# Four late weight-gradient stores on the software DMA ring, cut into pieces of rows

## The chip, the cores and the metric

The kernel runs on one core of one Trainium2 chip. The metric is the time of one execution on the device in microseconds (us); lower is better. Three executions of the kernel before took 409.05, 408.28 and 407.12 us, a median of 408.28. One more execution was recorded by the hardware profiler and took 407.01 us.

A core has five engines with instruction streams of their own: PE (matrix products), DVE and ACT (elementwise work), POOL and SP (here almost only issuers of transfers). Transfers between the memory of the chip and the core's own memory (128 partitions, "rows" below) are carried by sixteen DMA engines, which all issuers share. A store that POOL issues goes through the software ring (q0 in the profile), one from SP through q1, one from ACT through q10.

## The reference, cut to what matters

The reference computes a gated mix of two branches for one token, and then all gradients of it:

```python
def _A_ref(x, k_cache, v_cache, wq, wo):          # H=32 heads, Sk=4096 keys, Dh=128, D=640
    q = (x @ wq).reshape(B, Sq, H, Dh).transpose(0, 2, 1, 3)
    scores = jnp.einsum("bhqd,bhkd->bhqk", q, k_cache) * (Dh ** -0.5)
    p = softmax(scores, axis=-1)
    o = jnp.einsum("bhqk,bhkd->bhqd", p, v_cache)
    return o.transpose(0, 2, 1, 3).reshape(B, Sq, H * Dh) @ wo

def _B_ref(x, w1, b1, w2):                         # F=1728
    h = x @ w1 + b1
    return (h * tanh(softplus(h))) @ w2

g = sigmoid((x * gate_w).sum(-1, keepdims=True))
out = g * _A_ref(...) + (1 - g) * _B_ref(...)
_out, _vjp = jax.vjp(_f, x, k_cache, v_cache, wq, wo, w1, b1, w2, gate_w)
return (out, *_vjp(grad_out))
```

All tensors are bf16. The caches K and V have 32 MB each, and their gradients dK and dV have as much: every byte of K and V is read once and every byte of dK and dV is written once. Beside them stand wq and its gradient dwq (640 x 4096), wo and its gradient dwo (4096 x 640), and the small second branch (w1, w2 and theirs). Each of dK, dV, dwq and dwo is an outer product of two vectors, so that the work is mostly moving bytes: 82.03 MB are read and 82.03 MB written.

## The kernel before, in words

The 32 heads are taken in 16 pairs (`NP`), and four pairs form a head group (`NG` = 4 groups of 8 heads). A pair's K is one tile of 128 partitions x 8192 elements (64 partitions for each head), and so is its V. There are seven such buffers (`bufs`, `kv0` to `kv6`). A V buffer is overwritten with dV in place, then stored, then free for the next load; a K buffer is treated in the same way. The list `loads` holds the loads in their order, and `pump` issues the next ones on SP's queue whenever a buffer is free. wq lies whole in one tile (`wqa`, 128 partitions x 5 x 4096: input row 5p + r lies in partition p), and dwq is written into it in place. wo is loaded one head group at a time into two buffers (`wob`, 128 x 8 x 640), and dwo is written over it.

The order of the work is written out by hand. The main loop runs over pairs i and, within a pair, over 16 slots s; `slot(i, s)` issues a fixed part of the attention work (transposes, products, softmax, the outer products `outer` on DVE and the stores `store_kv`), and then the functions that a table `side` holds for (i, s). `plan` and `at` fill that table. The store of dK goes out at slot 3 of the next pair and that of dV at slot 13: on POOL's queue as long as there are loads left, on SP's queue after that. The last pair (i = 15) is written out behind the loop: its dV and dK go out in halves on SP (`last_dv`, `last_dk`), dwo of the last head group in two halves on ACT.

What the change touches:

- `st_dwo(g, eng, ...)` stores dwo of a head group. For group 2 (the third), it is planned at pair 13, slot 0, on POOL (line 689): one store of 128 partitions, 10,240 bytes in each.
- `st_dwq(c0, c1, eng)` stores a range of columns of dwq. The columns of group 2 (1024 of them) go out at pair 14, slot 6, on POOL (line 702): 128 partitions with five runs of 2048 bytes each. The first 512 columns of group 3 go out at pair 15, slot 3, on POOL (line 709), and its last 512 columns behind the loop on POOL (line 902), between `last_dk(1)` and `last_dk(2)`: 128 partitions with five runs of 1024 bytes each.
- The three short outputs (`frow`, line 934) are issued last, on POOL too.

Four more things bear on the order in which POOL issues: its stream is served in order; every store waits for the engine that made its data; the ring's stores use eight completion semaphores in turn, so that a store also waits until the one eight places before it has landed; and loads on SP wait for the store that empties their buffer.

Of the kernel before, what the change touches and what calls it, by code (L numbers as in the profile page):

```python
# [17 lines left out]
def kernel(  # L18
# [33 lines left out]
    nc = tc.nc  # L52
    P = 128
# [8 lines left out]
    GC = 8 * Dh  # L62
# [10 lines left out]
    HC = 2 * GC  # L73
# [7 lines left out]
    dwq_v = out_4.rearrange("(p r) c -> p r c", r=RC)  # L81
    wo_v = A_wo.rearrange("(g p k) n -> g p k n", p=P, k=8)
    dwo_v = out_5.rearrange("(g p k) n -> g p k n", p=P, k=8)
# [24 lines left out]
    wqa = big.tile([P, RC, H * Dh], BF16, name="wq", tag="wq")  # L108
    wob = [big.tile([P, 8, D], BF16, name=f"wo{i}", tag=f"wo{i}") for i in range(2)]
# [242 lines left out]
    def dwo_row(g, k, eng=nc.scalar):  # L352
        scaled(eng, wob[g % 2][:, k, :], da_bc[:], o8f[:, k:k + 1])

    def st_dwo(g, eng, k0=0, k1=8):
        eng.dma_start(dwo_v[g][:, k0:k1], wob[g % 2][:, k0:k1])


    def kview(b):
# [127 lines left out]
    def dwq_row(g, c0, c1, rc, eng=nc.scalar):  # L487
        scaled(eng, wqa[:, rc, g * GC + c0:g * GC + c1], dqrow[g % 2][:, c0:c1], xf[:, rc:rc + 1])

    def st_dwq(c0, c1, eng):  # L490
        eng.dma_start(dwq_v[:, :, c0:c1], wqa[:, :, c0:c1])


    hT = C([P, FN], F32, "hT")
# [123 lines left out]
    def at(i, s, f, *a):  # L618
        side.setdefault((i, s), []).append(lambda: f(*a))

    def plan(i, table):
        for s, tasks in table.items():
            for t in tasks:
                at(i, s, *t)

    def dx(g, part, c0, c1, *rcs):
        return [(dx_sum, g, part, c0, c1, rc) for rc in rcs]
# [42 lines left out]
    for k in range(8):  # L670
        at(4, (6, 7, 9, 10, 11, 11, 13, 14)[k], dwo_row, 0, k, nc.vector if k in (4, 5, 6, 7) else nc.scalar)
    plan(4, {5: rows(mlp_dxb, 0), 7: rows(mlp_dxb, 1), 14: rows(mlp_dxb, 2)})
    plan(5, {0: [(st_dwo, 0, nc.gpsimd)], 1: [(ld_wo, 2)], 5: rows(mlp_dxb, 3), 7: rows(mlp_dxb, 4), 14: dx(0, 0, 0, GC, 0)})
    plan(4, {10: [(ld_wq, HC, 2 * HC, nc.scalar)]})
    plan(6, {0: [(st_dw1,)]})

    for g in range(NG - 1):
        i = 4 * g + 4
        if g:
            plan(i - 1, {14: [(o_dup, g)]})  # L680
            plan(i, {0: [(o_rows, g)], 2: [(a_cols, g, 0, 2)], 3: [(a_cols, g, 2, 4)], 4: [(a_cols, g, 4, 5)]})
            if g + 2 < NG:
                for k in range(8):
                    at(i, 5 + k // 4, dwo_row, g, k, nc.vector)
                plan(i, {7: [(st_dwo, g, nc.gpsimd)], 15: [(ld_wo, g + 2)]})
            else:
                for k in range(8):
                    at(i, (5, 6, 7, 9, 10, 12, 13, 14)[k], dwo_row, g, k)
                plan(i + 1, {0: [(st_dwo, g, nc.gpsimd)]})
        for k, (j, s) in enumerate((((1, 14), (2, 5), (2, 6), (2, 7), (2, 14)), ((1, 5), (1, 7), (2, 5), (2, 7), (2, 14)),  # L690
                                    ((0, 14), (1, 5), (1, 6), (1, 7), (1, 14)))[g]):
            if (g, k) != (0, 0):
                plan(i + j, {s: dx(g, g, 0, GC, k)})
            at(i + j, s + 1 if s < 15 else s, dwq_row, g, 0, GC, k)
    for g in (2, 3):
        i = 4 * g
        q_prep(i - 1, 2, g)
        plan(i - 2, {15: sums(g, 0)})
        plan(i - 1, {4: sums(g, 1), 5: sums(g, 2, 3), 6: sums(g, 4, 5), 7: sums(g, 6, 7)})
        do_prep(i - 1, 8, g)  # L700
    plan(12, {8: [(st_dwq, 0, HC, nc.scalar)]})
    plan(14, {6: [(st_dwq, HC, HC + GC, nc.gpsimd)]})

    CA, CB = GC // 2, 3 * GC // 4
    g, i = NG - 1, NP - 2
    for k, s in enumerate((5, 6, 7, 14, 15)):
        plan(i, {s: dx(g, g, 0, CA, k)})
        at(i, s + 1 if s < 15 else s, dwq_row, g, 0, CA, k)
    at(i + 1, 3, st_dwq, g * GC, g * GC + CA, nc.gpsimd)
    plan(i + 1, {4: dx(g, NG, CA, CB, 0, 1, 2), 5: dx(g, NG, CA, CB, 3, 4)})  # L710


# [144 lines left out]
    i, g = NP - 1, NG - 1  # L857
# [9 lines left out]
    def last_dk(t):  # L867
        outer(fb, st[i]["ds"], Qr[g % 2][:, q, :], t)
        if t % 2:
            h = slice((t - 1) * KVW // 4, (t + 1) * KVW // 4)  # L870
            nc.sync.dma_start(dKv[i][:, h], bufs[fb][:, h])
# [27 lines left out]
    for rc in range(RC):  # L899
        dx_sum(g, NG + g, CB, GC, rc)  # L900
        dwq_row(g, CB, GC, rc)
    st_dwq(g * GC + CA, (g + 1) * GC, nc.gpsimd)
    last_dk(2)
    last_dk(3)

# [58 lines left out]
```

## Time and profile before

| What | Value |
|---|---|
| Median of three runs | 408.28 us (407.12 to 409.05) |
| The profiled execution | 407.01 us, of which its instructions span 405.2 us |
| PE, DVE, ACT, POOL busy | 74%, 70%, 61%, 6% of the span |
| Bytes moved | 164.88 MB, 407 GB/s on average |
| Queue q1 (SP), share of the sixteen DMA engines' time | 55.7% |
| Queue q0 (POOL, software ring) | 37.4% |
| Queue q10 (ACT) | 4.0% |
| Third group's dwo (1280 KB), issued on POOL | 322.98 us |
| Third group's dwq (1280 KB), issued on POOL | 341.59 us |
| Fourth group's first half of dwq (640 KB), issued on POOL | 363.98 us |
| Fourth group's second half of dwq (640 KB), issued on POOL | 388.43 us |
| The short outputs (1.2 KB each), issued on POOL | 393.78 to 395.3 us |

The span runs from the first instruction to the last; around it lie 1.8 us of the execution's own time. The slices of the profile cut the span in 40 parts of 10.1 us and show each engine's busy share in tenths; its line "DMA" is the mean over the sixteen DMA engines, so that one engine busy alone shows as 0.06. A table by stretches has, behind the engines, the clock of PE, that mean share, and the GB/s moved. A line with "<-" names who ended a wait. "us to landing" is the time from the issue of a transfer until the last byte is reported. L and a number is a line of the kernel before.

### The profile page before, as it was taken

The page shows a single profiled execution, that of the slowest core. Times are in us where ns is not written, and L with a number is a line of the kernel's source. Part 1 is how long each engine was busy: PE and PEld are TensorE (multiplying, and loading weights), DVE is VectorE, ACT ScalarE, POOL GpSimd, SP SyncE. Part 2 cuts the span into 40 slices and gives each one's busy share as a digit, 9 for nine tenths or more (in the row PEclk, how much of TensorE's full clock was granted, in tenths as well). Part 3 has the DMA queues.
Part 4 walks back from the last instruction along what each step waited for, and adds up shares of the span by engine and source line. Part 5 has one row for each costly group of instructions (what it writes and reads, how often), then busy time and mean ns, then how long its engine had stood idle before and what let it go on. Part 6 is the DMA issues. An engine that isn't in the chain of part 4 may idle for free.

```text
span 405.2 us, 13019 instructions
## 1 busy us (share of the span) xinstructions
PE 301.1 (74%) x5643; PEld 278.8 (69%) x5646; DVE 285.5 (70%) x618; ACT 247.0 (61%) x507; POOL 25.1 (6%) x50
## 2 busy tenths in 40 slices
PE   3769898898886788792989879652989976787310
PEld 3548897877876778692789869652789776786200
DVE  2744969599984987864697949462695979497760
ACT  3444545477657778862667677651568996767520
POOL 3000000002000101000001000000000100000020
PEclk9886999899899889975999999895899999899555
DMA  8999999999999999999999999999999999999991
GB/s 263 429 401 429 422 421 420 429 413 362 389 427 427 415 415 426 424 432 424 432 432 420 430 425 426 429 422 437 428 425 407 424 426 421 415 432 416 387 412 61
DMA packets 15963, 164.88 MB, mean 407 GB/s; under 512 B 1713, under 2 KB 1905, under 8 KB 6178
## 3 DMA queue, kind: packets, MB, share of 16 engines
q1 hardware_dynamic: 8832, 94.08, 55.7%
q0 software_dynamic: 5472, 63.42, 37.4%
q10 hardware_dynamic: 1602, 6.56, 4.0%
q8 instruction: 44, 0.72, 0.7%
q14 instruction: 13, 0.11, 0.1%
HBM read 82.03 MB, written 82.03 MB: 405 GB/s over the span
## 4 chain that ended last, share of the span: by engine, by line
PE 29%; issue 24%; DMA 21%; DVE 15%; ACT 6%; POOL 2%; POOLq 0%; SPq 0%; ACTq 0%; DVEq 0%
PE tr L372 11%; DVE kv L463 7%; DMA out_dram<-kv 7%; DMA kv<-in_A_k_cache_dram 6%; DMA wo<-in_A_wo_dram 6%; PE dP L382 3%; PE dq L431 2%; PE S L382 2%; DMA wq<-in_A_wq_dram 2%; ACT tch L375 2%; PE o L431 2%; PE q_ps L275 2%; DVE junk L288 1%; PE a_ps L338 1%; PE h_ps L527 1%
## 5 line engine op out<-in xcount | busy, mean ns | idle before, releaser
L372 PE MATMUL tr<-idf,kv 128*128 128x128 f32 x1024 | 176.4, 300 | 33.9 <-DMA kv<-in_A_k_cache_dram 16.9
L375 ACT COPY tch<-tr 128x512 f32<-128x512 f32 x256 | 144.5, 587 | 82.9 <-PE tr L372 78.4
L372 PEld LDWEIGHTS tr<-idf,kv 128*128 128x128 f32 x1024 | 121.6, 153 | 40.7 <-issue 37.7
L382 PEld LDWEIGHTS <-tch 128*128 128x128 bf16 x2048 | 91.8, 100 | 24.8 <-ACT tch L375 19.8
L463 DVE TENSOR_TENSOR kv<-p_dup,Dr 128x2048 bf16<-128x2048 bf16 x64 | 76.6, 1219 | 4.6 <-ACT p_dup L422 4.2
L463 DVE TENSOR_TENSOR kv<-ds_dup,Qr 128x2048 bf16<-128x2048 bf16 x64 | 76.8, 1220 | 0.4
L431 PEld LDWEIGHTS <-kv 128*128 128x128 bf16 x2048 | 59.9, 98 | 6.0 <-issue 5.0
L382 PE MATMUL dP<-dR,tch 128*128 128x48 bf16 x1024 | 48.9, 187 | 8.8 <-ACT tch L375 8.4
L382 PE MATMUL S<-qR,tch 128*128 128x48 bf16 x1024 | 48.1, 187 | 6.1 <-ACT tch L375 5.3
L431 PE MATMUL dq<-ds_m,kv 128*128 128x48 bf16 x1024 | 31.2, 183 | 5.4 <-issue 2.9
L288 DVE SCALAR_TENSOR_TENSOR junk<-wo,da_bc 128x640 bf16<-128x640 bf16 x32 | 26.3, 822 | 11.3 <-DMA wo<-in_A_wo_dram 10.6
L431 PE MATMUL o<-e_m,kv 128*128 128x48 bf16 x1024 | 32.6, 187 | 0.0
L734 POOL DMA_DIRECT2D out_dram<-kv x25 | 13.4, 535 | 296.4 <-DVE kv L463 236.5
L350 ACT ACTIVATE wq<-dqrow,xf 128x1024 bf16<-128x1024 bf16 (+2 forms) x30 | 25.1, 860 | 1.2 <-DVE wq L484 0.8
L484 DVE SCALAR_TENSOR_TENSOR wq<-wq,dqrow 128x1024 bf16<-128x1024 bf16 (+2 forms) x30 | 25.1, 863 | 0.2
L437 DVE TENSOR_TENSOR o<-o,rz 128x2 f32<-128x2 f32 x16 | 2.5, 158 | 31.1 <-PE o L431 31.1
L422 ACT ACTIVATE p_dup<-e_m,rz 64x128 bf16<-64x128 bf16 x32 | 12.7, 397 | 7.8 <-DVE rz L416 7.4
L350 ACT ACTIVATE wo<-da_bc,o8f 128x640 bf16<-128x640 bf16 x20 | 15.9, 825 | 1.5 <-PE a_ps L338 1.0
L404 DVE TENSOR_REDUCE negM<-mt 64x1 f32<-64x64 f32 x32 | 7.1, 222 | 12.2 <-PE mt L401 11.6
L396 DVE TENSOR_REDUCE m<-S 64x1 f32<-64x64 f32 x32 | 7.0, 219 | 12.0 <-PE S L382 11.7
L478 PE MATMUL dqr_ps<-idb,dqb 128*128 128x128 bf16 x32 | 4.9, 240 | 13.1 <-DVE dqb L475 13.1
L457 ACT COPY ds_dup<-ds_m 64x128 bf16<-64x128 bf16 x32 | 9.5, 296 | 8.2 <-DVE ds_m L453 7.6
(161 smaller groups left out, 251.1 us busy)
## 6 DMA issues: line engine op xcount, KB each, us to landing
out_dram<-kv POOLq DMA_DIRECT2D x25, 2048.0 KB, 19.4
kv<-in_A_v_cache_dram SPq DMA_DIRECT2D x16, 2048.0 KB, 19.7
kv<-in_A_k_cache_dram SPq DMA_DIRECT2D x15, 2048.0 KB, 20.2
out_dram<-kv SPq DMA_DIRECT2D x5, 2048.0 KB, 26.2
wo<-in_A_wo_dram SPq DMA_DIRECT2D x4, 1280.0 KB, 21.1
out_dram<-kv SPq DMA_DIRECT2D x4, 1024.0 KB, 16.5
out_dram<-wo POOLq DMA_DIRECT2D x3, 1280.0 KB, 27.0
wq<-in_A_wq_dram SPq DMA_DIRECT2D x2, 1280.0 KB, 9.5
```

The lines of the kernel that those rows point to most:

```text
L275: nc.tensor.matmul(ps[:].rearrange("p a h d -> p (a h d)"), lhsT=xc[:, rc:rc + 1].to_broadcast([P, P]), rhs=wqa[:, rc, g * GC + a * 512:g ...
L288: nc.vector.scalar_tensor_tensor(junk[:], in0=wob[g % 2][:, k, :], scalar=1.0, in1=da_bc[:], op0=ALU.mult, op1=ALU.mult, accum_out=do8[g % ...
L350: nc.scalar.mul(dst, src, col)
L372: nc.tensor.transpose(tp[:, t, :], src[:, 4 * c + t, :], idf[:])
L375: nc.scalar.copy(dst[:].rearrange("p a b e -> p (a b e)").bitcast(F32), tp[:].rearrange("p a b -> p (a b)"))
L382: nc.tensor.matmul(ps[:, 4 * B:4 * B + W].rearrange("p (a b) -> p a b", b=4), lhsT=src[:, t, :, e], rhs=col[:, e, :, :].rearrange("p a b - ...
L422: nc.scalar.activation(p[HS[hh]], e_m[i % 2][HS[hh], :, hh].unsqueeze(2).to_broadcast([64, J, 2]), ACT.Copy, scale=st[i]["rz"][HS[hh], hh: ...
L431: nc.tensor.matmul(st[i][key][:].rearrange("p (a b) -> p a b", b=2), lhsT=src[:, j, :], rhs=rhs[:, j, :].unsqueeze(1).to_broadcast([P, W / ...
L457: nc.scalar.copy(ds[HS[hh]], ds_m[i % 2][HS[hh], :, hh].unsqueeze(2).to_broadcast([64, J, 2]))
L463: nc.vector.tensor_tensor(kview(b)[:, j0:j0 + n, :].rearrange("p j (a b) -> p j a b", b=2), col[:, j0:j0 + n, :].unsqueeze(2).to_broadcast ...
L484: nc.vector.scalar_tensor_tensor(w, in0=w, scalar=1.0, in1=dqrow[g % 2][:, c0:c1], op0=ALU.mult, op1=ALU.mult, accum_out=dq_acc[:, rc, par ...
L734: eng.dma_start(dst, bufs[b][:, 0:J * Dh])
```

## The change

`st_dwo` and `st_dwq` get an argument `rows`, a list of counts of partitions that add up to 128. They issue one store for each count, on the same queue, one after the other; together the pieces write the bytes that the one store wrote. Without the argument they do what they did. Four calls use it:

- dwo of the third group: 5, 120 and 3 rows
- dwq of the third group: 14, 105 and 9 rows
- the first half of dwq of the fourth group: 8 and 120 rows
- the second half: 9, 8, 105 and 6 rows

POOL thus issues twelve stores in place of four. Every other instruction is the same, and stands in the same order.

```diff
-    def st_dwo(g, eng, k0=0, k1=8):
-        eng.dma_start(dwo_v[g][:, k0:k1], wob[g % 2][:, k0:k1])
+    def st_dwo(g, eng, k0=0, k1=8, rows=(P,)):
+        p0 = 0
+        for n in rows:
+            eng.dma_start(dwo_v[g][p0:p0 + n, k0:k1], wob[g % 2][p0:p0 + n, k0:k1])
+            p0 += n
...
-    def st_dwq(c0, c1, eng):
-        eng.dma_start(dwq_v[:, :, c0:c1], wqa[:, :, c0:c1])
+    def st_dwq(c0, c1, eng, rows=(P,)):
+        p0 = 0
+        for n in rows:
+            eng.dma_start(dwq_v[p0:p0 + n, :, c0:c1], wqa[p0:p0 + n, :, c0:c1])
+            p0 += n
...
-                plan(i + 1, {0: [(st_dwo, g, nc.gpsimd)]})
+                plan(i + 1, {0: [(st_dwo, g, nc.gpsimd, 0, 8, (5, 120, 3))]})
...
-    plan(14, {6: [(st_dwq, HC, HC + GC, nc.gpsimd)]})
+    plan(14, {6: [(st_dwq, HC, HC + GC, nc.gpsimd, (14, 105, 9))]})
...
-    at(i + 1, 3, st_dwq, g * GC, g * GC + CA, nc.gpsimd)
+    at(i + 1, 3, st_dwq, g * GC, g * GC + CA, nc.gpsimd, (8, 120))
...
-    st_dwq(g * GC + CA, (g + 1) * GC, nc.gpsimd)
+    st_dwq(g * GC + CA, (g + 1) * GC, nc.gpsimd, (9, 8, 105, 6))
```

## The prediction, made before the changed kernel was run

> **What bounds the kernel now.** I read the span and the slices first, then the queues, then the issues of the four stores, then the last ten microseconds in steps of one, then what the ending waits for.
>
> ```profile
> span 405.2 us, 13019 instructions
> DMA  8999999999999999999999999999999999999991
> GB/s 263 429 401 429 422 421 420 429 413 362 389 427 427 415 415 426 424 432 424 432 432 420 430 425 426 429 422 437 428 425 407 424 426 421 415 432 416 387 412 61
> q1 hardware_dynamic: 8832, 94.08, 55.7%
> q0 software_dynamic: 5472, 63.42, 37.4%
> ```
>
> From the second slice to the last but one the sixteen DMA engines are over 90% busy and move some 420 GB/s, while PE, DVE and ACT are at 61 to 74% of the span: transfers set the pace. Only the last slice (395.1 to 405.2) is empty. By microsecond, with DMA share and GB/s as the last two columns:
>
> ```profile
> 394.00:395.00 1.00, 0.00 (x0) 0.00 (x0) 0.00 (x0) 0.00 (x0) 1.00 (x3) 0.50 1.03 395
> 395.00:396.00 1.00, 0.00 (x0) 0.00 (x0) 0.00 (x0) 0.00 (x0) 0.31 (x1) 0.50 0.78 298
> 396.00:397.00 1.00, 0.00 (x0) 0.00 (x0) 0.00 (x0) 0.00 (x0) 0.00 (x0) 0.50 0.37 149
> 397.00:398.00 1.00, 0.00 (x0) 0.00 (x0) 0.00 (x0) 0.00 (x0) 0.00 (x0) 0.50 0.21 83
> 398.00:399.00 1.00, 0.00 (x0) 0.00 (x0) 0.00 (x0) 0.00 (x0) 0.00 (x0) 0.50 0.07 25
> 402.00:403.00 1.00, 0.00 (x0) 0.00 (x0) 0.00 (x0) 0.00 (x0) 0.00 (x0) 0.50 0.06 25
> ```
>
> A share of 0.06 is one engine of sixteen, at 25 GB/s, and it is alone for over 5 us. SP's ending waits for it: first for the last dwq store, then 5.2 us more for a store of dK.
>
> ```profile
> SPq L959 <- DMA out_dram<-wq: 10.1, 1, 10.1
> SPq L959 <- DMA out_dram<-kv: 5.2, 1, 5.2
> ```
>
> The packet records of the trace name no engine, but a packet begins where the one before it on its engine ends, so that they can be laid into sixteen unbroken sequences. In these one engine is late: its last packet ends at 403.46, the next at 398.20, 397.83, 397.37 and 397.26, the other eleven by 396.5. At 391.3 it has 25 packets of 8 KB (205 KB) more to do on SP's queue than the engines that lead. It is slow all along: from 130 us its 16 KB packets take 654 ns on the software ring and 634 on SP's queue, against 613 to 622 and 611 to 620 on the others. The last landings, 0.4 us behind the packets, are 403.89 for it and 399.2 for the next. Its row sums agree: 25 stores of 128 rows left 3200 packets of 16 KB, thus 8 rows an engine, equal for all.
>
> The four stores, on POOL:
>
> ```profile
> 322.98 0.53 POOL L356 DMA_DIRECT2D out_dram<-wo  x1 [1.98 <-ACT wo L350]
> 341.59 0.85 POOL L491 DMA_DIRECT2D out_dram<-wq  x1 [18.08 <-ACT wq L350]
> 363.98 0.84 POOL L491 DMA_DIRECT2D out_dram<-wq  x1 [21.55 <-ACT wq L350]
> 388.43 0.82 POOL L491 DMA_DIRECT2D out_dram<-wq  x1 [23.61 <-ACT wq L350]
> 393.78 1.53 POOL L934 DMA_DIRECT2D out_dram<-frow  x3 [4.52 <-DVE frow L931]
> ```
>
> All lie in the last 83 us, and POOL waits in front of each.
>
> **The change, part by part.** No compute moves and no byte is added. Four issues become twelve, in POOL's order, at the same places.
>
> *Issues.* Two more at 323 (0.53 us each), two at 341.6, one at 364 and three at 388.4 (0.85 each at most): 5.3 us of POOL, which is 6% busy. The first three lie in POOL's own waits of 18.1, 21.6 and 23.6 us. The last group ends at 388.43 + 4 x 0.85 = 391.8, and frow is ready at 393.5: 1.7 us of cover. Without it each further issue would put out_0, out_1 and out_9 back by 0.85; they land at 400.3 by the records, 3.6 us ahead of the end. Each ring store also waits that the one eight before it has landed. The pieces bring that forward: the fourth piece at 388.4 waits for the first at 341.6, which in the kernel before landed as a whole by 367; frow's three wait for pieces issued by 364, landed by 378. Nothing. Nor does SP pass or meet a new wait: it loads and stores in the old order. **Sum: 0**, at most 1.
>
> *Who carries the rows.* The trace shows equal shares of 128 rows only; no store of 5, 105 or 120 rows is in it. Bounds: spread evenly (no effect); on few engines (a loss, below); or equal shares with a whole engine left out. Between them I take the row that is nearest, the 128 rows as 8 on each. 120 is 15 x 8 and 105 is 15 x 7: in equal whole shares each leaves one engine of sixteen out. If shares are dealt in turn, one engine after the other, the pieces ahead of the large ones (5; then 5+15+3+14 = 37; 37+15+9+8 = 69; 69+15+9+8 = 101) begin each large piece at the sixth engine from the start (5, 37, 69 and 101 are all 5 more than a multiple of 16). So all four large pieces leave out the same engine, the fifth. It gets 2, 2, 1 and 3 rows in place of 8. A row is 10.24 KB (dwo; dwq of 1024 columns) or 5.12 KB (512 columns): 6 x 10.24 + 6 x 10.24 + 7 x 5.12 + 5 x 5.12 = 184 KB less on it, and on average 184/15 = 12.3 KB more on each of the others, never above one row in a store (30.7 KB in all).
>
> *If the fifth is the late engine.* Relief: 184 KB at 25.1 GB/s (16 KB in 654 ns) = 7.3 us, so that it would land at 396.6. Then others are last: 399.2 plus 12.3 KB at 26.7 GB/s (16 KB in 614 ns) = 0.46, thus 399.7. The ending moves by 403.9 - 399.7 = **-4.2 us**. On the way the loads, which wait for stores to land in SP's queue (26 waits, 287.6 us in total), come up to 2.4 us earlier after the first store, but the other engines have no free time to use it in, save in the stretch from 380 to 384 (share 0.93 and 0.84, 0.46 us idle). The floor is perfect balance: the shares after 395 add up to 1.7 us of all engines, an end at 396.7 in place of 403.46, -6.7 us.
>
> *Sum.* The profiled execution took 407.01 (its span of 405.23 and 1.8 around it): 407.0 - 4.2 = 402.8. It lies 1.3 under the median of the three runs, 408.28; from the median 404.1, and with a little of the stretch at 380 **404.0 us**.
>
> [...]
>
> **The rivals.**
>
> *1. The engine left out is not the late one.* No view numbers the engines, so nothing excludes it. The late engine then keeps its 8 rows or gets one more in some stores: 0 to 30.7 KB, 0 to 1.2 us, on average 0.5. Time 408.3 to 409.5, likeliest 408.8: no change that can be measured (within 0.5%, 2.0 us, is about what a measurement of this kernel can't tell from none). For it: fifteen places out of sixteen are wrong ones, and the engine left out could differ from one execution to the next if the dealing goes on where the last one stopped (the pieces add up to 122, which is 10 over a multiple of 16). Against it: the amount left out, 184 KB, is near the 205 KB that the late engine is behind, sizes that agree only if the two have to do with one another.
>
> *2. Slower: the large pieces go on few engines.* That shape decides is shown: dwo in 128 rows went out 8 rows an engine, but the one-row store at L602 left a single packet of 3456 bytes. With 120 rows on eight engines and 105 on seven, each of these has 15 rows for 8: 7 x 10.24 x 2 + 7 x 5.12 x 2 = 215 KB more, 8.1 us. On engines that are not late: 399.2 + 8.1 = 407.3, +3.4, thus 411.7; with the late one among them +8.1, thus 416. It decides as soon as an engine has over 4.7 us (125 KB) too much. Against it: the 64-row store of dW2 went over all sixteen.
>
> *3. The tail moves, but less.* The late engine's relief at 323 and 341.6 is eaten by 388, since it gets new loads as soon as old ones land; only the last two stores' 61 KB (2.4 us) stay. Time 405.9. Against it: its backlog grows from stage to stage, which means that it keeps what it owes.
>
> **How the numbers follow.** The forecast 0.54, with its own range 402.0 to 405.5 (-6.3 to -2.8); rival 3 0.07; rival 1 0.26; rival 2 0.09; 0.04 for loss by pieces that I don't see, such as three more issues that put frow behind the end. The first is a judgement on one open question, which engine is left out; size speaks for it, numbering is silent. Faster by over 0.5% (under 406.2): 0.54 and most of rival 3, 0.60. Slower (over 410.3): rival 2, the rest and the top of rival 1, 0.14. Same: 0.26. The range goes from 401.8, under which I leave 0.03, to 410.0, over which I leave 0.15.
>
> **What would show it.** Right: in the last slices the DMA share falls from 1.0 to nothing within 3 us, no stretch of 0.06 over 2 us; SP's last wait for a dK store shrinks from 5.2 to about 1; landings of SP's loads after 345 come nearer to those of the other fifteen engines; POOL has twelve issues, all done by 392. Wrong: a tail of 0.06 as long as before (rival 1), or several engines busy after 400 (a share of 0.4, rival 2). The forecast fails if the dealing starts elsewhere or a piece is not dealt in whole equal shares.

## The result, and the profile after

The changed kernel takes 409.59 us (median of 20 runs, 407.01 to 412.43) against 407.88 for the kernel before (20 runs, 406.01 to 410.43): ratio 1.0053, 95% interval 1.0035 to 1.0071, thus some 2.2 us slower. The forecast was 404.0 us and faster. The range (401.8 to 410.0) holds the time; the direction is wrong. The first rival (408.3 to 409.5, the engine left out is not the late one) came nearest.

The page after, its slices and the two large queues:

```profile
span 406.2 us, 13027 instructions
DMA  8999999999999999999999999999999999999992
GB/s 281 422 410 429 429 414 426 426 428 423 424 426 409 392 423 427 424 431 431 431 423 428 426 429 422 429 423 433 427 393 387 423 422 412 424 393 382 384 386 85
q1 hardware_dynamic: 8832, 94.08, 55.9%
q0 software_dynamic: 5808, 63.42, 37.6%
```

The engines are as busy as before, but in the four slices ahead of the last they move 393, 382, 384 and 386 GB/s, where the kernel before had 432, 416, 387 and 412. All queues together were busy for 97.9% of 405.2 us, 396.7 us of each engine; now (55.9 + 37.6 + 4.1 + 0.7 + 0.1 = 98.4% of 406.2) for 399.7. The same 164.9 MB cost 3.0 us more.

The last microseconds after, DMA share and GB/s in the last two columns:

```profile
394.00:395.00 1.00, 0.00 (x0) 0.00 (x0) 0.00 (x0) 0.00 (x0) 0.93 (x2) 0.50 1.00 316
395.00:396.00 1.00, 0.00 (x0) 0.00 (x0) 0.00 (x0) 0.00 (x0) 0.00 (x0) 0.50 0.96 302
396.00:397.00 1.00, 0.00 (x0) 0.00 (x0) 0.00 (x0) 0.00 (x0) 0.00 (x0) 0.50 1.02 297
397.00:398.00 1.00, 0.00 (x0) 0.00 (x0) 0.00 (x0) 0.00 (x0) 0.00 (x0) 0.50 0.70 233
...
402.00:403.00 1.00, 0.00 (x0) 0.00 (x0) 0.00 (x0) 0.00 (x0) 0.00 (x0) 0.50 0.06 25
403.00:404.00 1.00, 0.00 (x0) 0.00 (x0) 0.00 (x0) 0.00 (x0) 0.00 (x0) 0.50 0.06 25
```

Two things stand here. The lone engine at 0.06 and 25 GB/s is still last. And from 394 to 397 all engines are busy at some 300 GB/s; before, a share of 1.03 at 394 moved 395. SP's ending waits for the same two stores as before, 13.1 and then 3.6 us (before 10.1 and 5.2): the others are later, the late one not earlier.

```profile
SPq L965 <- DMA out_dram<-wq: 13.1, 1, 13.1
SPq L965 <- DMA out_dram<-kv: 3.6, 1, 3.6
```

POOL's issues came as forecast, twelve stores in four groups, the last done 2.9 us ahead of the short outputs and with no wait between its pieces:

```profile
322.79 1.58 POOL L358 DMA_DIRECT2D out_dram<-wo  x3 [1.63 <-ACT wo L350]
341.48 2.10 POOL L496 DMA_DIRECT2D out_dram<-wq  x3 [17.11 <-ACT wq L350]
365.29 1.48 POOL L496 DMA_DIRECT2D out_dram<-wq  x2 [21.71 <-ACT wq L350]
387.95 2.56 POOL L496 DMA_DIRECT2D out_dram<-wq  x4 [21.19 <-ACT wq L350]
393.40 1.52 POOL L940 DMA_DIRECT2D out_dram<-frow  x3 [2.89 <-DVE frow L937]
```

**Who carried the rows.** The packet records bear out the shares: 31 packets of 1024 bytes, which is 8 + 9 + 8 + 6 (the small pieces of the fourth group's two dwq stores, one engine for each row), 38 of 2048 (14 + 15 + 9) and 15 of 3072 (the last store's piece of 105 rows, on fifteen engines). (A share of dwq went in packets of 4096 bytes, 602 of them on the ring, before 640, and a last one for the rest; these are the last ones.) An engine without rows in a piece was not passed over: for each packet that an engine with rows moved it ran a small one, of 4 to 16 bytes; besides 4 bytes for each engine and each of the eight more stores, the trace after has 75 more packets of 4 bytes than the one before, 35 more of 8, one of 12 and 51 of 16, in all 162, as many as that makes over the twelve pieces. But the engine that was left out was not the late one. The sixteen landings of dwo's 120 rows (us from the start of the span, as all times here):

```
339.56 342.34 342.61 342.76 343.21 343.34 343.35 343.87 344.00 344.09 344.32 344.81 344.89 345.19 346.23 351.74
```

339.56 is the engine without rows; 351.74 is the late engine, which had its eight. It is last in the stores of dK, dV and dwq from there on, and ends at 404.88 (before 403.89). In its sequence of packets at the end it has a row of the piece of 9, none of the 8, seven of the 105 and none of the 6. Followed back to 318 us, that is one of the places 10 to 12 of the dealing (counted from 0), not place 4 (the fifth). At these it carries one row of 10.24 KB more in all: 0.4 us.

**What the packets cost.** From the packet records, the time of the larger packets (1 KB and more), per KB, in the stretches of the late dwq stores, and the mean busy time of the sixteen engines over the whole execution:

```
                        356 to 380        392 to 404
kernel                  ring    SP queue  ring    SP queue   busy, us
before                  40.7    38.4      43.1    38.8       396.4
after                   53.3    41.3      55.3    44.2       399.5
after, once more        51.3    42.3      56.1    43.9       400.2
even pieces             55.1    39.7      59.1    45.3       399.9
halves of 64            56.1    41.3      66.0    42.2       401.0
halves of 64, again     55.2    41.8      67.4    41.8       402.6
every other row         40.3    38.5      45.0    39.0       395.8
halves by columns       40.6    38.5      44.9    39.5       396.7
                        (ns a KB)
```

The rows below "after" are experiments, told next. In the changed kernel, the even pieces and the halves of 64, the stores' own packets take 26 to 56% longer than before, and SP's packets beside them 3 to 17% longer.

### The profile page after: what moved, and what is told of

Same layout as the page of the kernel before. It is cut to its first block, busy times and chain, and to the rows that moved or that the text cites. A ratio compares the mean times of both kernels' runs of the same rounds, so it can differ in the third digit from the quotient of the medians.

```text
span 406.2 us, 13027 instructions
## 1 busy us (share of the span) xinstructions
PE 298.7 (74%) x5643; PEld 277.4 (68%) x5646; DVE 285.7 (70%) x618; ACT 247.2 (61%) x507; POOL 29.7 (7%) x58
## 3 DMA queue, kind: packets, MB, share of 16 engines
q1 hardware_dynamic: 8832, 94.08, 55.9%
q0 software_dynamic: 5808, 63.42, 37.6%
## 4 chain that ended last, share of the span: by engine, by line
issue 43%; DMA 18%; PE 17%; DVE 13%; ACT 4%; POOL 2%; POOLq 0%; SPq 0%; DVEq 0%; ACTq 0%
DMA kv<-in_A_k_cache_dram 11%; DVE kv L466 7%; PE tr L375 6%; DMA out_dram<-kv 5%; DMA wq<-in_A_wq_dram 2%; PE o L434 2%; POOL out_dram L740 2%; PE dP L385 1%; PE S L385 1%; ACT tch L378 1%; PE q_ps L275 1%; PE dq L434 1%; PE h_ps L533 1%; PE a_ps L338 1%; DVE wq L487 1%
## 5 line engine op out<-in xcount | busy, mean ns | idle before, releaser
L487 DVE SCALAR_TENSOR_TENSOR wq<-wq,dqrow 128x1024 bf16<-128x1024 bf16 (+2 forms) x30 | 25.1, 862 | 0.2
L412 ACT ACTIVATE e_m<-S,negM 64x64 bf16<-64x64 f32 x32 | 10.6, 330 | 6.8 <-DVE negM L407 6.1
```

The lines of the kernel that those rows point to most:

```text
L412: nc.scalar.activation(e_m[i % 2][HS[hh], :, hh], sview(S_ps[i], hh), ACT.Exp, bias=st[i]["negM"][HS[hh]], scale=1.0, accum_out=rs[i % 2][ ...
L487: nc.vector.scalar_tensor_tensor(w, in0=w, scalar=1.0, in1=dqrow[g % 2][:, c0:c1], op0=ALU.mult, op1=ALU.mult, accum_out=dq_acc[:, rc, par ...
```

## The experiments

Theory A: the late engine wasn't the one left out, and rows on the wrong engines are all that happened. Theory B: cutting a store by rows makes its packets slow by itself, whoever carries them. A third question is whether the relief would have worked, had it met the late engine.

**1. The changed kernel once more.**

> The changed kernel once more, for one more trace. In the first trace of it the packet records show the engine left out as the fifth from the start of the dealing, and the late engine as the eleventh, twelfth or thirteenth. If every execution begins the dealing at the same engine, the late engine is found in the same places again, and the tail of one engine at 0.06 is there again (about 4 to 6 us). If the dealing goes on from the execution before, the late engine is found elsewhere, the tail may be gone, and the time lies anywhere from 404 to 410 us.

One run: 407.57 us, span 405.7. The late engine is again not the one left out (of the 120 rows' landings the first is 339.76, the fifteenth 347.76 and the late one 350.65), and the last landing is 404.27. Its packets, followed back to 318 us, again fit the places 10 to 12 alone. So the miss is no single event.

**2. A probe of the dealing.** The last dwq store alone is cut:

```diff
-    st_dwq(..., nc.gpsimd, (9, 8, 105, 6))
+    st_dwq(..., nc.gpsimd, (2, 2, 2, 2, 2, 2, 2, 2, 3, 2, 2, 2, 2, 2, 99))
```

> A probe: the three earlier stores whole as before; the last dwq store alone is cut into 2 rows eight times, then 3, then 2 five times, then 99. Dealt in turn, the eight pairs go once round the sixteen engines, so that the trace shows in which pair the late engine stands: from the first trace of the change the sixth or seventh pair (places 11 to 13 of 16). If the dealing does not restart, any pair. Its time says little: fifteen issues at 0.85 us would put frow back to about 401, and 99 rows on eleven engines cost those up to 0.3 us: 407 to 412 us.

410.45 us (one run). The late engine has rows in two of the pairs with six others between, and nine rows of the 99: place 4 of the dealing, as its sequence of packets reads. In this kernel the forecast's engine was the right one; in the changed kernel it was not. The run also shows a wait which the forecast had named and found harmless, 2.37 us for the landing of the ring store eight before.

```profile
387.15 4.58 POOL L496 DMA_DIRECT2D out_dram<-wq  x8 [23.71 <-ACT wq L350]
394.10 0.58 POOL L496 DMA_DIRECT2D out_dram<-wq  x1 [2.37 <-DMA out_dram<-wq]
395.03 0.57 POOL L496 DMA_DIRECT2D out_dram<-wq  x1 [0.35 <-DMA out_dram<-wq]
```

Eight go out in one run, the ninth 2.37 us behind, and the 99 rows only at 399.71. The changed kernel with its twelve has none of this; kernels 9 and 11, told below, have the same wait with 2.44 and 2.53 us.

**3. Only dwo cut; all dwq stores whole.**

```diff
-    plan(14, {6: [(st_dwq, HC, HC + GC, nc.gpsimd, (14, 105, 9))]})
+    plan(14, {6: [(st_dwq, HC, HC + GC, nc.gpsimd, (128,))]})
```

(and so for the two late stores)

> Only dwo of the third group is cut (5, 120, 3); the three dwq stores are whole. Theory A, the wrong engine is left out and else nothing happens: no relief of the late engine, at most one row (0.4 us) more, thus ratio 1.000 to 1.001 against the kernel before. Theory B, the dwq pieces slow the packets down (in the first trace a KB on the software ring took 45 to 80 ns during them, 40 to 42 before): dwo's pieces did not (39 to 42 ns), so the loss of 0.5% goes away: 0.999 to 1.001. Rival C, any cut store costs about a quarter of the loss (issues, 4-byte packets for engines without rows): 1.0013.

Ratio 1.0002 (0.9984 to 1.0020): no change. The late engine wasn't the one left out here either (first landing of the 120 rows 340.07, last 351.22). The cost of the change thus comes with the dwq pieces.

**4. Everything cut, nobody left out.** All pieces are multiples of 16 rows:

```diff
-(5, 120, 3)   (14, 105, 9)   (8, 120)    (9, 8, 105, 6)
+(16, 96, 16)  (16, 96, 16)   (16, 112)   (16, 16, 80, 16)
```

> The same four stores cut into as many pieces, of 16, 96 and 16 rows, of 16, 96 and 16, of 16 and 112, and of 16, 16, 80 and 16: all multiples of sixteen, so that every engine keeps its 8 rows and none is left out. Theory A (only who carries the rows matters): 1.000. Theory B in the form that cutting dwq slows its packets whatever the shares: 1.004 to 1.006, with over 45 ns a KB on the ring during dwq. Theory B in the form that only unequal shares do it: 1.000, with 40 to 42 ns a KB.

Ratio 1.0025 (1.0002 to 1.0048), 408.21 us. In equal shares each engine has eight rows in each store, as before, and still the ring takes 55.1 ns a KB where it took 40.7. The end:

```profile
395.00:396.00 1.00, 0.00 (x0) 0.00 (x0) 0.00 (x0) 0.00 (x0) 1.00 (x3) 0.50 0.88 260
396.00:397.00 1.00, 0.00 (x0) 0.00 (x0) 0.00 (x0) 0.00 (x0) 0.16 (x1) 0.50 0.94 322
```

260 and 322 GB/s at shares of 0.88 and 0.94. Theory A alone falls: rows that go to no wrong engine cost some 1.0 us (0.1 to 2.0).

**5 to 7. Three tries at leaving out the late engine.** If the dealing began at the same engine in each program, kernels whose shares add up to a multiple of 16 would find the engine of place 4 or 5 again. In 5 and 6 a dV store of 2 MB is cut as well, so that the relief comes earlier and is larger.

```diff
+        for n in ((5, 120, 3) if dct is vbuf and i == 12 else (P,)):      (5; in 6: 6, 120, 2)
+            eng.dma_start(dst[p0:p0 + n], bufs[b][p0:p0 + n, 0:J * Dh])
 dwo of the third group: (14, 90, 24) in 5, (15, 75, 22, 16) in 6; all dwq whole
-    st_dwq(..., (9, 8, 105, 6))
+    st_dwq(..., (9, 8, 90, 18, 3))                                        (7; the rest as in the changed kernel)
```

> Two stores of large packets are cut in place of the four: dV of pair 12 (5, 120, 3 rows of 16 KB) and dwo of the third group (14, 90, 24 rows of 10 KB). The engines dealt add up to 23 + 41 = 64, four whole turns, so that every execution begins where the one before began; the fifth engine (place 4 from 0) gets 3 rows fewer than a half, 146 KB less than before, each other engine at most 16 KB more. The probe found the late engine in place 4, the two traces of the change in places 10 to 12 and 5 to 9. Theory P, the dealing goes on from one execution to the next (10 places a time in the change) and starts at 0 when the program is loaded: here the late engine is spared every time, the lone tail of 0.06 from 398 to 403 is gone, and the end comes 3.5 to 4.5 us earlier: ratio 0.989 to 0.992. Theory Q, its place is random in each execution: no gain on average, 0.999 to 1.002, and the tail is there in the profile with 15 chances in 16.

> The same two stores cut (6, 120, 2 and 15, 75, 22, 16), again four whole turns in sum, but the sixth engine (place 5) is spared 136 KB and place 4 gets 6 KB more. Theory P: the late engine is not the one spared; ratio 1.000 to 1.002, tail of 0.06 as before. Rival, cutting these stores helps whoever is spared: 0.989 to 0.992 here too.

> The changed kernel with one edit: the last store goes out as 9, 8, 90, 18, 3 rows in place of 9, 8, 105, 6, so that the engines dealt add up to 128 in place of 122 and the next execution begins at 0 again. Theory P: the late engine is spared 143 KB every time and no longer last; what is left is the slower packets of the cut dwq (3.0 us of all engines in the first trace of the change, 98.4% of 406.2 against 97.9% of 405.2): 403.5 + 3.0 - 6.0, but not below the others at about 400.4: ratio 0.992 to 0.996. Theory Q: as the change, 1.004 to 1.007.

All three missed: 1.0085 (1.0055 to 1.0115), 1.0083 (1.0055 to 1.0111) and 1.0066 (1.0035 to 1.0096). In none was the late engine the one left out: in 5 the first of the 120 rows' landings is 329.21 and the late one is last with 345.47; in 6 329.64 and 344.86; in 7 one engine is alone from 402 to 406 (share 0.06) and lands at 407.08. What they do show is the price of a cut in a store that loads wait for. In the traces before and of kernel 5, by stretches of 4 us:

```profile
332.00:336.00 4.00, 4.00 (x93) 3.95 (x91) 2.87 (x7) 3.58 (x6) 0.00 (x0) 1.00 1.00 419
336.00:340.00 4.00, 3.64 (x100) 3.50 (x99) 3.94 (x7) 2.72 (x6) 0.00 (x0) 1.00 1.03 438
```

```profile
332.00:336.00 4.00, 3.40 (x58) 2.91 (x55) 3.60 (x9) 3.92 (x8) 0.00 (x0) 1.00 1.04 269
336.00:340.00 4.00, 3.76 (x102) 3.60 (x99) 4.00 (x5) 2.08 (x6) 0.00 (x0) 1.00 0.89 319
```

269 GB/s in place of 419 at about the same share. The three pieces of the dV store land at 330.59, 345.47 and 347.31 (the whole store before at 340.26), and the load of V that waits for them is issued at 347.51 in place of 340.38.

**8. Cut by columns.** The third group's dwq in two halves of 512 columns, each of 128 rows; nothing else cut.

```diff
+    plan(14, {6: [(st_dwq, HC, HC + GC // 2, nc.gpsimd), (st_dwq, HC + GC // 2, HC + GC, nc.gpsimd)]})
```

> No rows are cut; the dwq store of the third group goes out as two column halves of all 128 rows (1024-byte runs, as the later dwq stores have). It asks why a KB on the ring took 45 to 80 ns during the cut dwq stores. If the cut by rows does it (each engine then reads other rows than in a store of 128): 40 to 43 ns a KB here. If two stores of one tensor at a time, or the shorter runs, do it: 45 ns and more. Time 407 to 408.5 us.

407.44 us (one run, before 407.10). While the two halves are on their way (342 to 368 us) the ring takes 40.0 ns a KB, and 40.1 before. Two stores in place of one, with runs of half the length, did not make slow packets here; pieces of rows did (55.1 in kernel 4).

**9 to 11. Does the dealing go on from kernel to kernel?** The same kernel twice, with one between that ends its dealing seven engines on.

```diff
+    st_dwq(..., (2, 2, 2, 2, 2, 2, 2, 2, 112))     (9 and 11; the other stores whole)
+    st_dwq(..., (8, 120))                          (10; the other stores whole)
```

> dwo of the third group and the first two dwq stores whole; the last dwq store in eight pieces of 2 rows and one of 112. Every ring store of this kernel uses a multiple of 16 shares in sum (8 x 2 = 16, the rest 16 each), so the dealing ends an execution where it began. The late engine carries a row in exactly one of the eight pairs, which its packets show. If the dealing begins at the same engine in every execution, it is the third pair (place 4), as in the probe. If it goes on where the execution before stopped, any pair. Time about 409 to 410.5 by the probe (410.45), whose ring stores waited for landings too.

> The last dwq store alone in 8 and 120 rows, the other three whole: 8 + 15 = 23 shares, so the dealing ends 7 engines on after each execution. By itself: 407.5 to 409 (one store cut, one engine left out of it). Its use is to shift the dealing between the kernel before this one and the one behind it.

> The kernel with eight pairs once more. Dealing that begins anew in each execution: the late engine in the same pair as two kernels earlier. Dealing that goes on: in another pair, 7 engines times the number of executions of the kernel between away.

408.43, 408.64 and 410.69 us (one run each). In 9 and in 11 the late engine has its row in the third pair, place 4 or 5; in 10 it has a row of the 8 and eight of the 120, one of the places 0 to 6. That is what a fresh start in each execution would give, and it fits kernel 2. It doesn't fit the changed kernel (10 to 12 in both traces), unless its executions do not begin where the others do; nor can I exclude that the dealing went on and came round. Kernels 5 to 7, on another chip, left out places 4 and 5 and missed. Where the dealing starts is left open.

**12. Plain halves.**

```diff
-(5, 120, 3)   (14, 105, 9)   (8, 120)   (9, 8, 105, 6)
+(64, 64)      (64, 64)       (64, 64)   (64, 64)
```

> All four stores in two halves of 64 rows: eight issues, 4 rows on each engine in each, no engine left out, no small pieces. If a store is slow because each engine reads other rows than in a store of 128 rows (4e to 4e+3 in place of 8e to 8e+7), the ring's packets take 45 to 80 ns a KB in the stretch from 340 to 395 as in the changed kernel, the DMA share stays at 1.0 with about 300 GB/s at 394 to 397, and the ratio is 1.002 to 1.006. If the small pieces (3 to 16 rows) or the share dealt on 15 engines make it, the packets stay at 39 to 42 ns a KB and the ratio is within 0.2% of 1.

Ratio 1.0025 (1.0003 to 1.0048); ring 56.1 and 66.0 ns a KB. Two pieces of four rows an engine made packets as slow as small and odd pieces did (53.3 and 55.3 after). Theory B holds without any of the change's particular numbers.

**13 to 16. One of four must hit.** Third group's dwo and dwq are cut into p, 108 and 20 - p rows; 108 rows lie on twelve engines (twelve packets of 2048 bytes in dwq, beside 20 of the single rows), so that four neighbours (places p - 4 to p - 1) carry 2 rows a store and the others 10. The late dwq stores are whole.

```diff
+(p, 108, 20 - p) for both, with p = 4, 8, 12, 16
```

> Third group's dwo and dwq in 4, 108 and 16 rows, the two late dwq stores whole. 108 rows lie on twelve engines with 9 rows each; places 0 to 3 get 2 rows in all per store, the other twelve 10, in place of 8. If the late engine is at place 0 to 3: 123 KB less on it, 4.9 us, and 41 KB more on the others, 1.6 us: last landings at about 399 for it and 400.8 for the others, ratio 0.990 to 0.998 if the relief is kept, 1.000 or more if slower packets eat it. If it is not: 41 KB more on it, 1.6 us, and the 0.5 to 1 us of a cut by rows: ratio 1.004 to 1.009.

> The same with 8, 108 and 12 rows: places 4 to 7 get 2 rows per store. Late engine there: 0.990 to 0.998 if the relief is kept; not there: 1.004 to 1.009. If the dealing began at the same engine in every execution, and the late one were at place 4 as in the probe, it would be this kernel.

> The same with 12, 108 and 8 rows: places 8 to 11 get 2 rows per store. Late engine there: 0.990 to 0.998 if the relief is kept; not there: 1.004 to 1.009.

> The same with 16, 108 and 4 rows: places 12 to 15 get 2 rows per store. Late engine there: 0.990 to 0.998 if the relief is kept; not there: 1.004 to 1.009.

Ratios 1.0015 (0.9992 to 1.0038), 0.9993 (0.9967 to 1.0019), 1.0042 (1.0021 to 1.0063), 1.0027 (1.0008 to 1.0046). The second looks like the hit. The lag of a dK store's last lander behind the fifteenth, and the two last landings of all (us):

```
                     13      14      15      16
dK store near 385    5.4     1.4     5.1     5.7     last behind the 15th
last dK store, 15th  400.61  401.65  399.27  400.59
last dK store, last  405.97  402.99  404.10  405.40
```

The end of kernel 14 and of kernel 15:

```profile
398.00:399.00 1.00, 0.00 (x0) 0.00 (x0) 0.00 (x0) 0.00 (x0) 0.00 (x0) 0.50 0.32 132
399.00:400.00 1.00, 0.00 (x0) 0.00 (x0) 0.00 (x0) 0.00 (x0) 0.00 (x0) 0.50 0.30 124
400.00:401.00 1.00, 0.00 (x0) 0.00 (x0) 0.00 (x0) 0.00 (x0) 0.00 (x0) 0.50 0.22 91
401.00:402.00 1.00, 0.00 (x0) 0.00 (x0) 0.00 (x0) 0.00 (x0) 0.00 (x0) 0.50 0.06 25
```

```profile
400.00:401.00 1.00, 0.00 (x0) 0.00 (x0) 0.00 (x0) 0.00 (x0) 0.00 (x0) 0.50 0.06 25
401.00:402.00 1.00, 0.00 (x0) 0.00 (x0) 0.00 (x0) 0.00 (x0) 0.00 (x0) 0.50 0.06 25
402.00:403.00 1.00, 0.00 (x0) 0.00 (x0) 0.00 (x0) 0.00 (x0) 0.00 (x0) 0.50 0.06 25
```

SP's last wait for a store of dK, in 14 and then in 15:

```profile
SPq L965 <- DMA out_dram<-kv: 1.5, 1, 1.5
```

```profile
SPq L965 <- DMA out_dram<-kv: 4.7, 1, 4.7
```

In 14 the long tail of one engine is gone: three to five engines (0.22 to 0.32) share the end, and SP's wait for the last dK store is 1.5 in place of 4.7 us. A short tail alone proves nothing, for the halves of kernels 12 and 18, which spare no engine, end with lags of 1.6 and 0.5 us: there the others come late. What tells them apart is the last lander's own time, from the last landing of the K load near 352 to that of a dK store near 378: 24.8 us in 14, 27.6 to 28.2 in its three sisters, 27.6 and 27.7 in the halves. So taking rows off the late engine does bring it forward by some 3 us, and this lasts to the end.

The relief is smaller than worked out, though. Through dwo's 108 rows the last lander gains nothing on the sisters (8.9 us, theirs 8.5 to 9.1); what it gains comes with dwq's, and 2.8 to 3.4 us are one store's eight rows (82 KB, 3.3 us at 25.1 GB/s), not the 123 KB of two. Since the trace names no engine, whether it was spared in one store only is not shown. And the others end at 401.65, where 41 KB more (1.6 us) from 399.2 gave 400.8, the late one at 402.99 where I had 399: part of the shorter lag is that the others are later, by 1.0 to 2.4 us than in the sisters. The last landing is 0.9 us ahead of that of the kernel before, and the time is the same within 0.3%.

**17 and 18. Why rows.** All four stores in halves again: of every other row, and beside it, on the same chip, of 64 neighbours.

```diff
+        for a in (0, 1):
+            eng.dma_start(dwq_v[a::2, :, c0:c1], wqa[a::2, :, c0:c1])      (17; dwo alike)
+(64, 64)                                                                   (18, for all four)
```

> [...] If the rows' places on the engines make the packets slow: 39 to 42 ns a KB on the ring from 356 to 396, as before, DMA share and GB/s at the end as before, ratio 0.999 to 1.001. If the number of stores or the form of a 64-row store makes it: 45 to 75 ns a KB, ratio 1.002 to 1.005.

> The halves of 64 neighbouring rows once more, beside the halves of every other row on one chip: 45 to 75 ns a KB on the ring from 356 to 396, ratio 1.002 to 1.004 (1.0025 in the first measurement).

1.0011 (0.9996 to 1.0025) for every other row, 1.0027 (1.0006 to 1.0048) for neighbours. The intervals overlap, so the two times are not told apart; the packets are: 40.3 against 55.2 ns a KB on the ring, 45.0 against 67.4 at the end. The stretches of the fourth group's first half, kernel 17 and then kernel 18:

```profile
368.00:372.00 4.00, 2.98 (x92) 2.79 (x92) 1.93 (x11) 2.05 (x5) 0.00 (x0) 1.00 1.01 427
372.00:376.00 4.00, 2.21 (x65) 2.10 (x65) 1.36 (x2) 2.40 (x6) 0.00 (x0) 0.80 1.02 423
```

```profile
368.00:372.00 4.00, 2.89 (x87) 2.69 (x86) 1.33 (x9) 1.45 (x4) 0.00 (x0) 1.00 0.97 318
372.00:376.00 4.00, 1.20 (x41) 1.09 (x41) 1.45 (x3) 2.49 (x7) 0.00 (x0) 1.00 1.03 367
```

The same number of stores, of rows and of bytes, at shares of 0.97 to 1.03: 427 and 423 GB/s against 318 and 367. So here it is which rows a store holds that sets the price of its packets, not how many stores there are. Why is not shown. The expectations of kernels 8 and 12 name a reading, that in 64 neighbours an engine reads other rows than in a store of 128; in every other row it would then keep to its own. The two kernels agree with it, but it is my guess: the trace names neither the engine nor the rows of a packet. Nor does it take halves: pieces of 105 and 120 rows are slow too (in kernel 10, where only the last store is cut, into 8 and 120, the ring takes 57.0 ns a KB from 392 to 404, before 43.1). The reason is left open.

## Why the prediction was wrong, point by point

- **What bounds the kernel: right.** Transfers set the pace, and one late engine ends last: the last dK store's last landing is 2.4 to 9.0 us behind its fifteenth in every trace but those of kernel 14 (1.3) and of the halves of 64 (1.6 and 0.5).
- **Issues, sum 0: right.** Eight more issues on POOL met no wait; the kernels with nine pieces and more in one store did (2, 9 and 11).
- **Who carries the rows: right in the shares, one row or several rows an engine and fifteen engines for 105 and 120.** The forecast took this from "equal shares dealt in turn", and the counts of packets bear it out (31 of 1024 bytes, 38 of 2048 and 15 of 3072). Other counts of rows went in equal whole shares too, on fewer engines: the 108 rows of kernels 13 to 16 left 32 packets of 2048 bytes, which is twelve engines' shares of dwq's 108 rows and 20 single rows; the 99 rows of kernel 2 left 40 packets of 1024 bytes and none of 3072, which is eleven engines' shares of nine rows and 29 single rows.
- **"If the fifth is the late engine": the step that failed.** It sat at one of the places 10 to 12. The forecast gave this case 0.54 because 184 KB is near the 205 KB that the engine is behind; that nearness meant nothing. The argument against, fifteen wrong places out of sixteen and a dealing that may shift, was in the text and got 0.26. The late engine kept its rows and got one more, and its last landing came 1.0 us later, not earlier.
- **"No byte is added": true, and the second failure.** The sum priced rows and issues but not the packets, which took 53.3 for 40.7 ns a KB on the ring and put 3.0 us of busy time on each engine. Halves and even pieces, with every engine at its old number of rows, cost some 1.0 to 1.1 us (ratios 1.0025, 1.0025, 1.0027). No row of the trace before holds a store of other than 128 or 64 rows of that size, and I gave the term no bounds at all, where a loss could not be excluded.
- **Rival 1: right in its kind, at 408.3 to 409.5, but by too small a sum.** It had 0.5 us for rows. Of the 2.2 us measured (1.4 to 2.9), 0.4 are the late engine's extra row and about 1.0 a cut by rows as such; the rest, some 0.8, I can't assign, and it is within the intervals.
- **The size of the relief, -4.2 us: not borne out.** Kernel 14 was to take 123 KB, 4.9 us, off the late engine. The lag fell by 3.7 to 4.3 us, in part since the others were later; the last lander itself gained some 3 us, its last landing was only 1.1 to 3.0 us ahead of those of the three sisters, and the time no better than before. A changed kernel that hit the late engine wasn't run.
- **Rival 3** (relief eaten by new loads) is not borne out: the lag that kernel 14 took off was still off at the end, some 19 us later. **Rival 2** (few engines) fell by the packet counts.

## What to carry to other kernels

When transfers bound a kernel, don't take a store to be free to cut as long as its bytes stay the same. Here halves by columns and of every other row kept the packets as they were (40.0 and 40.3 ns a KB on the ring, before 40.1 and 40.7), and halves of 64 neighbours took 55 to 67. Look at GB/s against DMA share, which showed slow packets (318 GB/s at 0.97) where the share alone showed full engines. A plan that needs one certain engine to be left out must first show, in a trace, that the dealing meets that engine each time. A term of the sum that has no row in the trace needs a bound on the loss side even where "nothing is added".

## What the runs showed of the hardware

- In kernels 12 and 18, stores of 64 neighbouring rows took 55 to 67 ns a KB on the ring beside SP's traffic, in kernel 17 those of every other row 40 to 45; SP's packets beside the former took 8 to 9% longer than before.
- The cut was dear in dV (16 KB a row: 269 GB/s for 419) and in dwq (53.3 ns a KB for 40.7), and not measurable in the time for dwo alone (ratio 1.0002, 0.9984 to 1.0020).
- An engine without a share in a ring store was not passed over: it ran a small packet, of 4 to 16 bytes, for each one that an engine with rows moved (162 in the changed kernel).
- In both traces of the changed kernel the late engine's place in the dealing was 10 to 12; in others it was 4 (kernel 2) or 4 or 5 (9 and 11), and kernel 14 points to 4 to 7. The trace names no engine, so whether it is the same one on every chip is not shown.
